# Turning all of B by transposing transfers in halves, moving two small loads to ScalarE's queue, and a new instruction order, in a kernel of two sequence layers

## The chip, the cores and the metric

The kernel runs on one core of one Trainium2 chip. The metric is the device time of one execution in microseconds (us); the figure given for a kernel is the median of its runs.

Engines are called PE (TensorE), DVE (VectorE), ACT (ScalarE), POOL (GpSimd) and SP (SyncE, whose queue issues most transfers). PEld is PE's loading of weights.

## What is computed

Two layers over 2048 positions and 640 channels, all in bf16, written side by side into one output of 2048 x 1280.

```python
# layer A: a diagonal complex recurrence
Lam_bar = exp(exp(log_dt) * Lam)
B_bar   = ((Lam_bar - 1) / Lam)[:, None] * (B_re + 1j * B_im)
Bu      = einsum("bld,pd->blp", x, B_bar)
for t in range(2048):  h = Lam_bar * h + Bu[:, t];  hs.append(h)
y_A     = 2 * real(einsum("blp,dp->bld", hs, C_re + 1j * C_im)) + x * Dskip

# layer B: a short convolution, a gate, a convolution as long as the sequence, a gate
kv  = (sum over t of 4 shifts of k times shift_k) * v
y   = irfft(rfft(kv, 4096) * rfft(ssm_k, 4096))[:2048] + kv * ssm_D
y_B = q * y
```

## The kernel before, in words

**Layer A.** The 640 states are five blocks of 128, called j = 0 to 4; the 640 channels are five blocks too. Time is split into T = 8 phases c of M = 256 columns. x is loaded transposed, one transfer for each phase (`load_x`, L445), into tiles xT; phase c and phase c + 4 share a tile. B is needed transposed as well, in the tile BT with 2 parts (real r = 0, imaginary r = 1), five channel blocks and 640 state columns. For a block j the items `u1j`, `u3j` (phases 1 and 5, 3 and 7; one item for each part r), `vj` (phases 2 and 6), `wj` (phase 4) and `zj` (phase 0) multiply xT by BT on PE (L460, L468) and add, through small diagonal matrices diagL that hold powers of Lam_bar (L474, L475), what earlier phases gave. The results stand in PSUM and are copied into the tiles u by DVE (L148) or ACT (L146). After `zj` the scan `rsj` runs on DVE (L496, between rotations L487 to L489), then `roj`, then the seven other phases get the scanned state back: `mcj` multiplies (L316 on DVE, L314 on ACT) and `rcj` adds on DVE (L522). Last, 32 halves `pn_b` multiply the states by C on PE (L532). For n = 0, 1, 2 the skip term x * Dskip is added on PE, for the other 13 DVE adds it (L560, L547). Results go out from the tile yo.

**The parameters of layer A** come from four short loads on ACT's queue (`lv`, L151), one matmul that turns them (`pv`, L255), and long chains of five-column instructions on DVE: `rho`, `Fi` (to L280), `lam` (L293 to L310), and `gam` (L332 to L346). `dLj` builds diagL of block j, nine instructions.

**How B gets into BT.** Block 0 (128 rows, parts re and im) is loaded as it lies by two plain transfers on ACT's queue (`B0`, L155) into a corner of the tile zz. PE turns it by ten matmuls with the identity (`bt0_0`, `bt0_1`, L431 and L432), and DVE copies the result from PSUM into BT (`bte0_0`, `bte0_1`, L148). Blocks 1 and 2, and blocks 3 and 4, come by transposing transfers on SP's queue (`turn_B`, L167; items `B1` and `B3`, each a real and an imaginary transfer of 256 rows).

**Layer B** works in five groups G of 128 channels. For a group: k and v are loaded transposed (`kTG`, `vTG`, L584), a copy of k with halves exchanged is made (`ksG_h`, L148 or L146 into kS), the four taps run on PE (`tapG_m`, L617) with diagonals made from shift_k (`sk`, `dSG`), DVE multiplies by v (`kvG_m`, L622), the product goes out to DRAM and comes back in rows (`kvoG`, L625; `kvsG`, L595 into kv_st), and the filter's rows come in as `hsG` (L595 into h_st), to which DVE adds ssm_D (`hadG`, L601). Then three stages of a Fourier transform on PE with copies from PSUM between: `s1`, `s2` (L654), a complex product on DVE (`yG_h`, L668 to L671, some 3.8 us each), `inv` (L682), a turning transfer (`ztG`, L690), `fin` (L704), the gate on DVE (`obG`, L709) and the way out (`odG`).

**What sets the order.** There is no scheduler at run time. `make_plan` lists every item with engine, operands and a cost; a string ORDER, found beforehand from those costs, gives the order in which the items are issued, the pair of PSUM banks that an item uses (`@0` to `@7`), and for the copies and scalings that both can do, whether DVE (`v`) or ACT does them. Each engine and each queue runs its items strictly in that order and waits at each for its operands.

```python
    for n, _, how in names:              # names: ORDER.split()
        it = items[n]
        if it["eng"] == "AD":
            args.append("DVE" if how.endswith("v") else "ACT")
        ...
        it["fn"](*args)
```

Four warm-up items `wm0` to `wm3` (L422, four matmuls of 512 columns each with no use for their result) keep PE busy before operands come. Matrix C is loaded by two transposing transfers (`CT0`, `CT1`, L802) into Cs and scaled by `gam` in `caj` on ACT and `csj` on DVE. The vector ssm_D comes by two transfers on SP's queue into the zeroed tile dst (`dcol`, L570), and the taps shift_k by one (`l_sk`, L170).

Of the kernel before, what the change touches and what calls it, by code (L numbers as in the profile page):

```python
# [48 lines left out]
class Kernel:  # L49


    def __init__(self, ctx, tc, out, ins):
# [111 lines left out]
    def turn_B(self, j, n):  # L164
        s = slice(128 * j, 128 * j + 128 * n)
        for r, ap in enumerate((self.A_B_re, self.A_B_im)):
            self.nc.sync.dma_start_transpose(out=self.BT[:, r, :, s], in_=ap[s, :].rearrange("m (k d) -> m k d", d=128))  # L167
# [256 lines left out]
    def pe_bt(self, js, ks, ps):  # L424
        mm = self.nc.tensor.matmul
        i = 0
        for j in js:
            for k in ks:
                re, im = (self.Bn[:, r, j, 128 * k:128 * k + 128] for r in range(2))
                o_re, o_im = (ps[:, r, 128 * i:128 * i + 128] for r in range(2))  # L430
                mm(o_re, lhsT=re, rhs=self.ident[:], start=True, stop=True)  # L431
                mm(o_im, lhsT=im, rhs=self.ident[:], start=True, stop=True)  # L432
                i += 1

    def ev_bt(self, eng, js, ks, ps):
        n = len(js) * len(ks)
        if len(js) == 1:
            out = self.BT[:, :, ks[0]:ks[-1] + 1, 128 * js[0]:128 * js[0] + 128]
            self.copy(eng, out, ps[:, :, 0:128 * n].rearrange("p r (k n) -> p r k n", n=128))
        else:  # L440
            self.copy(eng, self.BT[:, :, ks[0], 128 * js[0]:128 * js[-1] + 128], ps[:, :, 0:128 * n])


# [580 lines left out]
```

## Time and profile before

| | |
|---|---|
| time of the kernel | median 194.97 us of 3 runs (194.75 to 196.81) |
| the profiled execution | 194.97 us, span 192.7 us |
| PE busy | 179.6 us (93%) |
| DVE busy | 175.0 us (91%) |
| ACT busy | 154.2 us (80%) |
| POOL busy | 20.0 us (10%) |
| SP's queue q1, packets' time as a share of 16 engines' span | 92.1% |
| transferred | 34.87 MB, mean 181 GB/s |

The span runs from the first instruction to the last; about 2.3 us of the execution lie around it. A row of a timeline gives the start, the length, the engine, the line, the operation, what it writes and reads, its shape, how many were merged, and in brackets how long the engine idled before it and what ended that. A row of the windows gives the stretch, its length, then busy time and count of instructions for PE, PEld, DVE, ACT and POOL, the clock granted to PE as a share of the full one, the share of time in which the transfer engines were busy, and GB/s. Rows of the issuing queue (SPq, ACTq) show how long the issue took, not when the data landed.

### The profile page before, as it was taken

What the parts mean: (1) busy time and instruction counts of PE and PEld (TensorE: products, weight loads), DVE (VectorE), ACT (ScalarE), POOL (GpSimd) and SP (SyncE); (2) the same over time, 40 slices, a digit from 0 to 9 for tenths busy, and PEclk for the clock granted to TensorE, in tenths of its full rate; (3) what the DMA queues carried; (4) which work ended last, traced back from release to release, by engine and by line L of the source; (5) the groups of instructions that cost most, each with busy time, mean ns of one, the idle gap of its engine ahead of it and who ended that gap; (6) DMA issues with size and microseconds to landing.
All of it is one profiled execution on the core that took longest, in us unless ns stands there. A gap on an engine that the chain in (4) does not pass through costs nothing. (4 is left out here: it accounts for less than half of the span.)

```text
span 192.7 us, 7254 instructions
## 1 busy us (share of the span) xinstructions
PE 179.6 (93%) x3135; PEld 121.6 (63%) x3135; DVE 175.0 (91%) x375; ACT 154.2 (80%) x220; POOL 20.0 (10%) x46
## 2 busy tenths in 40 slices
PE   6499999999898999999899997999999999999993
PEld 2334456556454668576565886787686878777761
DVE  2398799999999999999999999999999999999683
ACT  2648998999999999989899999899989968670000
POOL 8792283000000000000000000000000000000000
PEclk9859999999999999999999999999999999999999
DMA  4999999999999998999979998599935597359954
GB/s 92 183 200 155 190 175 235 229 151 246 189 168 248 177 218 147 156 266 205 189 127 178 126 280 201 111 170 176 228 106 143 114 193 234 102 151 230 256 157 135
DMA packets 131966, 34.87 MB, mean 181 GB/s; under 512 B 127200, under 2 KB 131296, under 8 KB 131936
## 3 DMA queue, kind: packets, MB, share of 16 engines
q1 hardware_dynamic: 131608, 34.10, 92.1%
q10 hardware_dynamic: 328, 0.33, 1.1%
q8 instruction: 24, 0.39, 0.8%
q14 instruction: 6, 0.05, 0.1%
HBM read 10.50 MB, written 7.86 MB: 95 GB/s over the span
## 5 line engine op out<-in xcount | busy, mean ns | idle before, releaser
L532 PE MATMUL banks<-Cs,u 128*128 128x320 bf16 x320 | 46.2, 299 | 0.3 <-DVE yo L547 0.3
L146 ACT CAST XH<-banks 128x1024 bf16<-128x1024 f32 x40 | 39.1, 1032 | 5.3 <-PE banks L654 5.3
L532 PEld LDWEIGHTS <-u 128*128 128x128 bf16 x320 | 30.2, 98 | 12.8 <-issue 0.5
L146 ACT CAST As<-banks 128x1024 bf16<-128x1024 f32 x38 | 37.6, 1043 | 0.8 <-PE banks L636 0.8
L460 PE MATMUL banks<-xT,BT 128*128 128x512 bf16 x150 | 37.4, 392 | 0.6 <-DVE u L148 0.6
L522 DVE TENSOR_TENSOR u<-tmp,u 128x1024 bf16<-128x1024 bf16 (+1 forms) x40 | 24.5, 623 | 1.0
L460 PEld LDWEIGHTS <-BT 128*128 128x128 bf16 x150 | 13.7, 100 | 17.9 <-issue 2.9
L146 ACT CAST u<-banks 128x512 bf16<-128x512 f32 x29 | 16.8, 594 | 6.0 <-PE banks L460 3.5
L146 ACT CAST zz<-banks 128x1024 bf16<-128x1024 f32 x20 | 20.2, 1035 | 1.6 <-PE banks L682 1.6
L654 PE MATMUL banks<-As,Gre 64*64 64x256 bf16 x320 | 19.4, 274 | 1.2 <-DVE As L148 0.8
L654 PE MATMUL banks<-As,Gim 64*64 64x128 bf16 x320 | 18.0, 216 | 0.0
L654 PE MATMUL banks<-As,nGim 64*64 64x128 bf16 x320 | 18.0, 216 | 0.0
L475 PE MATMUL banks<-u,diagL 128*128 128x256 bf16 (+1 forms) x60 | 15.9, 291 | 0.0
L474 PE MATMUL banks<-u,diagL 128*128 128x256 bf16 (+1 forms) x60 | 15.9, 290 | 0.0
L468 PE MATMUL banks<-xT,BT 128*128 128x256 bf16 x100 | 14.2, 273 | 0.7 <-DMA xT<-in_A_x_dram 0.6
L654 PEld LDWEIGHTS <-Gre 64*64 64x64 bf16 x320 | 10.2, 106 | 6.2 <-issue 4.0
L316 DVE TENSOR_SCALAR tmp<-u,lam 128x512 bf16<-128x512 bf16 (+2 forms) x45 | 13.7, 363 | 0.2
L709 DVE TENSOR_TENSOR qb<-banks,qb 128x1024 bf16<-128x1024 f32 x10 | 11.9, 1216 | 1.5 <-PE banks L704 1.5
L669 DVE TENSOR_TENSOR XH<-XH 128x2048 bf16<-128x2048 bf16 x10 | 12.2, 1225 | 0.4
L547 DVE TENSOR_TENSOR yo<-banks,BT 128x320 bf16<-128x320 f32 x26 | 11.8, 486 | 0.7 <-PE banks L532 0.2
L668 DVE TENSOR_TENSOR tmp<-XH 128x2048 bf16<-128x2048 bf16 x10 | 12.2, 1220 | 0.2
L622 DVE TENSOR_TENSOR vT<-banks,vT 128x1024 bf16<-128x1024 f32 x10 | 12.1, 1221 | 0.1
...
## 6 DMA issues: line engine op xcount, KB each, us to landing
...
```

What stands on the lines that cost most here:

```text
L146: self.nc.scalar.copy(out=out, in_=in_)
L316: self.nc.vector.tensor_scalar_mul(out=out, in0=in_, scalar1=w)
L460: self.nc.tensor.matmul(ps, lhsT=self.BT[:, r, k, j * 128:(j + 1) * 128], rhs=x[:, :, k, :], start=(k == 0), stop=(not joins and k == NT - 1))
L468: self.nc.tensor.matmul(o, lhsT=self.BT[:, r, k, j * 128:(j + 1) * 128], rhs=self.xc(c)[:, k, :], start=(k == 0), stop=False)
L474: mm(o, lhsT=self.dl(j)[:, 3 * s, :], rhs=src(c2, r), start=False, stop=False)
L475: mm(o, lhsT=self.dl(j)[:, 3 * s + 2 - r, :], rhs=src(c2, 1 - r), start=False, stop=(i == len(joins) - 1))
L522: v.tensor_tensor(out=o, in0=buf[:, i, 0:n], in1=o, op=ALU.add)
L532: mm(ps[:, 0:320], lhsT=h[:, r, ts], rhs=self.Cs[:, r, j, c0:c0 + 320], start=(j == 0 and r == 0), stop=(skip and j == NT - 1 and r == 1))
L622: self.nc.vector.tensor_tensor(out=self.vT[:, ts], in0=ps[:].rearrange("p a n -> p (a n)"), in1=self.vT[:, ts], op=ALU.mult)
L654: mm(out, lhsT=w[rows, k, :], rhs=rhs, start=(w is self.Gre), stop=(w is self.Gim))
L668: tt(out=cr, in0=X[:, :, ::-1, :], in1=pl(2, 3).to_broadcast([128, 8, 2, 128]), op=ALU.mult)
L669: tt(out=X, in0=X, in1=pl(0, 1).to_broadcast([128, 8, 2, 128]), op=ALU.mult)
```

## The change

Three things. B comes by transposing transfers alone: blocks 0 and 1, blocks 2 and 3, and block 4, each as one transfer for the real and one for the imaginary part, six items `Bj_r` on SP's queue; the ten matmuls, the two copies, the plain loads and their corner of zz are gone. A pair item of part r now waits for the transfers of its own part alone. The loads of shift_k and ssm_D are issued by ACT's queue. And the planner's costs were set anew (among them `rate=0.245` for transposing transfers, and higher costs of `Fi`, `lam`, `gam` and `dL`), and ORDER is a new one throughout. The choice of the three outputs whose skip term PE adds is written as a tuple `PD = (0, 1, 2)` in place of a count, with the same three.

```diff
-JB = 1
 NYO = 4
-NSK = 13
+PD = (0, 1, 2)
...
-    def turn_B(self, j, n):
+    def turn_B(self, j, n, r):
         s = slice(128 * j, 128 * j + 128 * n)
-        for r, ap in enumerate((self.A_B_re, self.A_B_im)):
-            self.nc.sync.dma_start_transpose(out=self.BT[:, r, :, s], in_=ap[s, :].rearrange("m (k d) -> m k d", d=128))
+        self.nc.sync.dma_start_transpose(out=self.BT[:, r, :, s],
+                                         in_=(self.A_B_re, self.A_B_im)[r][s, :].rearrange("m (k d) -> m k d", d=128))
...
-    def pe_bt(self, js, ks, ps):
...
-    def ev_bt(self, eng, js, ks, ps):
...
-        dma(name, "SP", cost, mb, deps, fn, lat=2.1, rate=0.228)
+        dma(name, "SP", cost, mb, deps, fn, lat=2.1, rate=0.245)
...
-    dma("B0", "ACT", 0.9, 0.36, ["lv"], lambda: K.load_B(nc.scalar, 0))
-    for j in (1, 3):
-        dmat(f"B{j}", 2.8, 0.655, (), lambda j=j: K.turn_B(j, 2))
+    for j, n in ((0, 2), (2, 2), (4, 1)):
+        for r in range(2):
+            dmat(f"B{j}_{r}", 1.45 if n == 2 else 1.3, 0.1638 * n, (), lambda j=j, n=n, r=r: K.turn_B(j, n, r))
...
-    dma("l_sk", "SP", 0.75, 0.06, (), lambda: K.load_sk(nc.sync))
+    dma("l_sk", "ACT", 0.65, 0.06, ["lv"], lambda: K.load_sk(nc.scalar))
...
-    dma("dcol", "SP", 1.0, 0.01, ["zd"], lambda: K.load_dcol(nc.sync))
+    dma("dcol", "ACT", 1.25, 0.01, ["zd", "lv"], lambda: K.load_dcol(nc.scalar))
...
-            pe(f"{nm}_{r}", n * P512, 2 * n, deps, lambda ps, r=r: K.pe_u(j, c, r, joins, ps), f"H{nm}_{r}")
+            pe(f"{nm}_{r}", n * P512, 2 * n, [d for d in deps if d[0] != "B" or d[-1] == str(r)], lambda ps, r=r: K.pe_u(j, c, r, joins, ps), f"H{nm}_{r}")
...
-        bt = [f"bte{j}_{x}" for x in range(2)] if j < JB else [f"B{(j - 1) // 2 * 2 + 1}"]
+        bt = [f"B{j // 2 * 2}_{r}" for r in range(2)]
...
-zer x5 pc lv B0 pc3 zd x7 pc2 dc wm1@0 gp0 wm3@2 wt dc2 pp pv@4 exp@4 vec@4 dD wm2@6 rho Fi gp2 bt0_0@0 rr trig1 hk tp0 tab0
...
+x1 zer pc dc lv pc3 x5 pc2 wm2@0 wm0@2 B0_0 wt B0_1 pv@4 exp@4 x7 zd wm1@6 dcol x3 wm3@0 dc2 i64 pp vec@4 hk rho rr pp2 Fi trig1
```

What the new order does is seen in the built programs, at three places. The first is the start of SP's queue, the transfers in the order of their issue. Tile xT_130 holds phases 1 and 5, xT_132 phases 3 and 7, xT_131 phases 2 and 6, xT_129 phases 0 and 4; dst belongs to ssm_D, sk_b to shift_k. Before:

```order
L445 DMA_TRANSPOSE xT_130<-in_A_x_dram 128x5x256
L445 DMA_TRANSPOSE xT_132<-in_A_x_dram 128x5x256 x2
L570 DMA dst<-in_B_ssm_D_dram 2x5x64 x2
L445 DMA_TRANSPOSE xT_130<-in_A_x_dram 128x5x256
L167 DMA_TRANSPOSE BT<-in_A_B_re_dram 128x5x256
L167 DMA_TRANSPOSE BT<-in_A_B_im_dram 128x5x256
L445 DMA_TRANSPOSE xT_131<-in_A_x_dram 128x5x256 x2
L445 DMA_TRANSPOSE xT_129<-in_A_x_dram 128x5x256
L584 DMA_TRANSPOSE kT<-in_B_k_dram 128x2048
L170 DMA sk_b<-in_B_shift_k_dram 128x5x4
L584 DMA_TRANSPOSE vT<-in_B_v_dram 128x2048
L445 DMA_TRANSPOSE xT_129<-in_A_x_dram 128x5x256
```

Now (the line numbers are those of the changed file):

```order
L419 DMA_TRANSPOSE xT_130<-in_A_x_dram 128x5x256 x2
L160 DMA_TRANSPOSE BT<-in_A_B_re_dram 128x5x256
L160 DMA_TRANSPOSE BT<-in_A_B_im_dram 128x5x256
L419 DMA_TRANSPOSE xT_132<-in_A_x_dram 128x5x256 x2
L160 DMA_TRANSPOSE BT<-in_A_B_im_dram 128x5x256
L419 DMA_TRANSPOSE xT_131<-in_A_x_dram 128x5x256 x2
L419 DMA_TRANSPOSE xT_129<-in_A_x_dram 128x5x256
L160 DMA_TRANSPOSE BT<-in_A_B_re_dram 128x5x256
L558 DMA_TRANSPOSE kT<-in_B_k_dram 128x2048
L558 DMA_TRANSPOSE vT<-in_B_v_dram 128x2048
L419 DMA_TRANSPOSE xT_129<-in_A_x_dram 128x5x256
```

Blocks 0 and 1 of B stand third and fourth, blocks 2 and 3 follow around phases 2, 6 and 4, and phase 0 of x, the last row of both, has four B transfers ahead of it where there were two and loads of dst and sk_b.

The second place is the same queue just behind, as far as the second load of kT (h_st: the filter's rows; kv_rows: the product on its way out; kv_st: the same coming back in rows; Cs: matrix C). Before:

```order
L595 DMA h_st<-in_B_ssm_k_dram 64x32x64 x2
L584 DMA_TRANSPOSE kT<-in_B_k_dram 128x2048
L625 DMA kv_rows<-vT 128x2048
L167 DMA_TRANSPOSE BT<-in_A_B_re_dram 128x5x256
L167 DMA_TRANSPOSE BT<-in_A_B_im_dram 128x5x256
L584 DMA_TRANSPOSE vT<-in_B_v_dram 128x2048
L595 DMA kv_st<-kv_rows 64x32x64 x2
L584 DMA_TRANSPOSE kT<-in_B_k_dram 128x2048
```

Now:

```order
L569 DMA h_st<-in_B_ssm_k_dram 64x32x64 x2
L768 DMA_TRANSPOSE Cs<-in_A_C_re_dram 128x5x640
L599 DMA kv_rows<-vT 128x2048
L558 DMA_TRANSPOSE kT<-in_B_k_dram 128x2048
L768 DMA_TRANSPOSE Cs<-in_A_C_im_dram 128x5x640
L558 DMA_TRANSPOSE vT<-in_B_v_dram 128x2048
L569 DMA kv_st<-kv_rows 64x32x64 x2
L558 DMA_TRANSPOSE kT<-in_B_k_dram 128x2048
L160 DMA_TRANSPOSE BT<-in_A_B_im_dram 128x5x128
```

Both parts of C come ahead of the first kv_st, where two transfers of B stood; before, C came after the second kv_st.

The third place is DVE between the end of `Fi` and the start of `lam`. Before:

```order
L279 TENSOR_SCALAR fr<-fr 128x5
L280 CAST Fi<-fr 128x5
L148 CAST BT<-banks 128x2x128
L148 CAST BT<-banks 128x2x4x128
L293 TENSOR_TENSOR lam<-rr,cos_86 128x5
```

Now:

```order
L273 TENSOR_SCALAR fr<-fr 128x5
L274 CAST Fi<-fr 128x5
L146 CAST u_134<-banks 128x2x256
L287 TENSOR_TENSOR lam<-rr,cos_86 128x5
L288 TENSOR_TENSOR lam<-rr,sin_84 128x5
```

Two copies of turned B into BT stood ahead of `lam`; now one copy of the first u item does.

More of the change, by code (lines that the diff above doesn't have):

```diff
@@ L422, in pe_warm @@
             self.nc.tensor.matmul(ps[:, i % 2, :], lhsT=self.ident[:], rhs=wide, start=True, stop=True)
-    def pe_bt(self, js, ks, ps):
[L425 to L433, printed above, removed]
-    def ev_bt(self, eng, js, ks, ps):
[L436 to L441, printed above, removed]
     def load_x(self, c):
@@ L549, in xr @@
     def xr(self, n):
-        return self.BT[:, 0, n % NXR, :]
+        return self.BT[:, 0, [k for k in range(16) if k not in PD].index(n) % NXR, :]
     def load_xr(self, c, i, n):
@@ L762, in make_plan @@
     dve("vec", 0.3, ["pv", "exp"], lambda ps: K.dve_vec(ps), give="pv")
-    dve("rho", 0.4, ["exp", "vec"], lambda: K.dve_rho())
+    dve("rho", 0.7, ["exp", "vec"], lambda: K.dve_rho())
     act("rr", 0.25, ["rho"], lambda: K.act_rr())
-    dve("Fi", 1.3, ["rho"], lambda: K.dve_Fi())
-    act("trig1", 2.1, ["Fi", "rr", "dc"], lambda: K.act_sincos())
-    dve("lam", 3.6, ["trig1", "rr"], lambda: K.dve_lam())
-    dve("gam", 1.8, ["lam"], lambda: K.dve_gamma())
+    dve("Fi", 1.9, ["rho"], lambda: K.dve_Fi())
+    act("trig1", 1.6, ["Fi", "rr", "dc"], lambda: K.act_sincos())
+    dve("lam", 4.8, ["trig1", "rr"], lambda: K.dve_lam())
+    dve("gam", 2.7, ["lam"], lambda: K.dve_gamma())
     gp("pc2", 1.6, ["pc"], lambda: K.pool_consts2())
@@ L786, in make_plan @@
         dve(f"nG{q}", 0.27, [f"G{q}"], lambda q=q: K.dve_nG(q))
-    bts = [(j, ks) for j in range(JB) for ks in ([0, 1, 2, 3], [4])]
-    for j, ks in bts:
-        x = int(ks[0] == 4)
-        w = len(ks)
-        pe(f"bt{j}_{x}", 2 * w * P128, 4 * w, ["dc", f"B{j}"],
-           lambda ps, j=j, ks=ks: K.pe_bt([j], ks, ps), f"bt{j}_{x}")
-        ev(f"bte{j}_{x}", 256 * w, [f"bt{j}_{x}"], lambda eng, ps, j=j, ks=ks: K.ev_bt(eng, [j], ks, ps), f"bt{j}_{x}")
-    bts_all = [f"bt{j}_{x}" for j in range(JB) for x in range(2)]
     gp("hk", 0.9, ["dc2"], lambda: K.pool_hk())
@@ L846, in make_plan @@
     zs_all = [n for j in range(NT) for n in both(f"u1{j}") + both(f"u3{j}") + both(f"v{j}") + [f"w{j}", f"z{j}"]]
-    if NSK:
+    if len(PD) < 16:
         dma("dbc", "SP", 0.5, 0.107, zs_all, lambda: K.load_dbc())
     seq = [(c, i) for c in (0, 4, 2, 6, 1, 5, 3, 7) for i in range(2)]
+    sk = [n for n in range(16) if n not in PD]
     for n, (c, i) in enumerate(seq):
         hs = [f"r{'o4'[c // 4] if c % 4 == 0 else c % 4}{j}" for j in range(NT)]
-        skip = n >= 16 - NSK
+        skip = n not in PD
         free = f"yd{n - NYO}" if n >= NYO else f"cs{NT - 1}"
         if skip:
-            dma(f"xl{n}", "SP", 0.43, 0.107, both(f"ye{n - NXR}") if n >= 16 - NSK + NXR else zs_all, lambda c=c, i=i, n=n: K.load_xr(c, i, n))
+            dma(f"xl{n}", "SP", 0.43, 0.107, both(f"ye{sk[sk.index(n) - NXR]}") if sk.index(n) >= NXR else zs_all, lambda c=c, i=i, n=n: K.load_xr(c, i, n))
             dve(f"xm{n}", 0.4, [f"xl{n}", "dbc"], lambda n=n: K.dve_xm(n))
```

80 lines of the change are left out of this document (38 added, 42 removed).

## Prediction

> **What bounds the kernel now.** I read the busy time by stretches first, then the timelines of DVE, PE and SP's queue. In the windows the columns after the length are PE, PEld, DVE, ACT and POOL, then PE's clock, the transfer engines' share and GB/s:
>
> ```profile
> 24.00:181.00 157.00, 151.69 (x2890) 107.35 (x2888) 153.14 (x278) 139.09 (x186) 5.61 (x9) 1.00 0.97 185
> ```
>
> For 157 us PE, DVE, ACT and the transfers are all close to full; DVE is the fullest, 153.1 of 157. Its timeline shows no wait above the view's threshold inside; these are the last wait ahead of the full stretch, the first instruction of the first scan, the last residual add, and the first wait behind:
>
> ```profile
> 23.86 0.80 DVE L148 COPY kS<-kT 64x1032 bf16<-64x1032 bf16 x1 [0.65 <-DMA kT<-in_B_k_dram]
> ...
> 33.02 0.42 DVE L487 TENSOR_TENSOR tmp<-tab,u 128x512 bf16<-128x512 bf16 x1
> ...
> 174.35 1.41 DVE L522 TENSOR_TENSOR u<-tmp,u 128x1024 bf16<-128x1024 bf16 x2
> ...
> 182.47 2.36 DVE L709 TENSOR_TENSOR qb<-banks,qb 128x1024 bf16<-128x1024 f32 x2 [1.50 <-PE banks L704]
> ```
>
> So three parts set the end: when the scan can start (33.02), how much DVE has to do from there to the last add (it ends at 175.8), and what PE has left then. The wait at 182 belongs to the tail, where PE is the bound.
>
> Ahead of 24 us the bound is what arrives. PE's start:
>
> ```profile
> 1.55 3.25 PE L422 MATMUL banks<-ident 128*128 128x512 bf16 x8 [1.55 <-DVE m_lo L207]
> ...
> 8.68 0.29 PE L432 MATMUL banks<-ident,zz 128*128 128x128 bf16 x1 [1.20 <-DMA zz<-in_A_B_im_dram]
> ...
> 11.47 10.31 PE L460 MATMUL banks<-xT,BT 128*128 128x512 bf16 x40
> ...
> 29.18 0.72 PE L468 MATMUL banks<-xT,BT 128*128 128x256 bf16 x5 [0.55 <-DMA xT<-in_A_x_dram]
> ```
>
> The first useful matmul stands at 11.47, behind the turning of block 0; at 29.18 z0 had waited 0.55 us for phase 0 of x. The first row also tells that the warm-up ran slowly: 8 matmuls of 512 columns in 3.25 us, 406 ns each. PE's clock, by stretches:
>
> ```profile
> 0.90:4.31 3.41, 2.76 (x7) 1.04 (x8) 0.92 (x15) 0.79 (x1) 3.33 (x14) 1.00 0.52 112
> 4.31:7.72 3.41, 1.68 (x8) 0.50 (x6) 0.95 (x6) 1.68 (x6) 3.01 (x9) 1.00 1.12 172
> 7.72:11.13 3.41, 2.45 (x13) 1.38 (x13) 2.23 (x8) 3.35 (x11) 2.40 (x5) 0.50 0.94 198
> 11.13:14.55 3.42, 3.42 (x9) 1.15 (x9) 3.38 (x18) 0.81 (x4) 3.25 (x5) 0.50 1.06 194
> ```
>
> The clock was half from 7.72 to 14.55 (and by the 406 ns also before 4.31, though no record says so). A stretch of 3.41 us with PE busy 81% (2.76) was followed by the full clock, one with 49% by the half, one with 72% (2.45) by the half again.
>
> **Block 0 of B off PE.** Ten matmuls and two DVE copies go (1215 and 425 ns, below). PE need not wait for them: the real half of blocks 0 and 1 is third in SP's queue.
>
> ```profile
> 3.85 2.91 SPq L445 DMA_TRANSPOSE xT<-in_A_x_dram  x1
> ...
> 6.88 1.29 SPq L570 DMA_DIRECT2D dst<-in_B_ssm_D_dram  x2
> ...
> 21.25 0.59 SPq L170 DMA_DIRECT2D sk_b<-in_B_shift_k_dram  x1
> ```
>
> The third transfer of before was issued at 3.85. The view of tile xT has the landing:
>
> ```profile
> DMA to landing us min/median/max: 5.0/5.2/6.7
> ```
>
> That makes 8.9 to 9.1. The plain load of block 0 ran beside it then:
>
> ```profile
> q10 hardware_dynamic: 328, 0.33, 1.1%
> ```
>
> 1.1% of 192.7 us is 2.1 us of all engines' time, which frees up. So the first u item starts between 7 and 9 us; the warm-ups last until about 8.3, and I take 8.7. PE is then busy for some 3.0 us of the stretch from 7.72 to 11.13, 88%, and I take the full clock from 11.13. Between the first u item and z0 PE had 17.2 us before (11.47 to 28.63, where z0's wait begins), 1.5 of it lost to the clock: 15.7 of work. Now two u halves more stand ahead of z0, (10.31 - 1.5) / 8 = 1.1 each, so 17.9 of work; 1.2 is lost to the clock. PE comes to z0 at 8.7 + 19.1 = 27.8. DVE's chain `lam` does not gain: the first u copy (686 ns) stands ahead of it and ends near 8.7 + 5 x 0.42 + 0.7 = 11.5, where before the copies of B ended at 11.4; its diagonals are needed by v0 only, at about 21, which hides it. Were that cover gone, v0 would slip by the 0.2 us.
>
> **When phase 0 of x lands.** Two more transposing transfers of 0.33 MB stand ahead of it. Transposes alone ran at
>
> ```profile
> 17.20:21.30 4.10, 4.10 (x21) 1.86 (x19) 3.76 (x28) 4.07 (x8) 0.00 (x0) 1.00 1.04 226
> ```
>
> 226 GB/s, so +2.9 us; the plain load frees 2.1. The two loads that moved to ACT's queue held SP's issue for 1.29 + 0.59 = 1.9 us. What that gave the transfers is between 0 (the engines had work left) and 1.9; I take 1.0, the middle, since the stretch from 6.88 on lay behind transfers still under way. Sum: 29.2 + 2.9 - 2.1 - 1.0 = 29.0, bounds 28.1 and 30.0. On ACT's queue the loads cost the same 1.9 us, ssm_D's ahead of `rr`, which waits for `rho` anyway, shift_k's ahead of copies that PE's slower start delays.
>
> The Trainium skill (DMA: Bandwidth & Descriptors, "Issuing engines are not separate DMA queues") says that transfers issued by several engines share the same 16 transfer engines and that spreading them saves issue time only. By that alone the sum would be 30.0; the transfer share of 0.97 above agrees with it.
>
> So z0 starts at 29.0, by its operand, and not by PE (27.8). The scan stood 3.84 us behind z0's start, of which DVE's own work held the last 0.6, for the copy of z0 ended at 32.4:
>
> ```profile
> 31.80 0.58 ACT L146 CAST u<-banks 128x512 bf16<-128x512 f32 x1 [0.74 <-PE banks L475]
> ```
>
> Now DVE has less ahead of the scan (next part), so 29.0 + 3.2 = 32.2: **-0.8 us**.
>
> **What DVE has to do.** By the order's rows, with these durations:
>
> ```profile
> L148 DVE CAST u<-banks 128x512 bf16<-128x512 f32 x11 | 7.4, 686 | 0.9 <-PE banks L460 0.5 <-ACT Gre L142 0.4
> ...
> L148 DVE COPY kS<-kT 64x1032 bf16<-64x1032 bf16 x7 | 3.3, 477 | 0.8 <-DMA kT<-in_B_k_dram 0.6
> L148 DVE CAST As<-banks 128x1024 bf16<-128x1024 f32 x2 | 2.5, 1226 | 0.1
> ...
> L148 DVE CAST BT<-banks 128x1024 bf16<-128x1024 f32 x1 | 1.2, 1215 | 0.0
> ...
> L148 DVE CAST BT<-banks 128x256 bf16<-128x256 f32 x1 | 0.4, 425 | 1.0 <-PE banks L432 1.0
> ```
>
> and of the timeline
>
> ```profile
> 36.84 0.74 DVE L316 TENSOR_SCALAR tmp<-u,lam 128x512 bf16<-128x512 bf16 x3
> ...
> 38.99 1.01 DVE L316 TENSOR_SCALAR tmp<-u,lam 128x1024 bf16<-128x1024 bf16 x3
> ...
> 47.28 1.55 DVE L316 TENSOR_SCALAR diagL<-ident,lam 128x128 bf16<-128x128 bf16 x9
> ```
>
> Over the whole kernel DVE loses the two copies of B (1.6), six u copies (4.1), two long and one short set of scalings (2.0 + 0.7), and gains three kS copies (1.4), one set of diagL (1.6) and one copy out of PSUM of 1024 columns (1.2): 4.2 us net, all but the first shifted to ACT or taken from it; ACT's 139 of 157 us leave room for that. But nearly all of it goes ahead of the scan: there the two B copies, two u copies and some smaller ones go, a kS copy and the diagL come, about 3 us less. From the scan to the last add four copies (-2.7) and the scalings (-2.7) go, and two kS copies, one copy of 1024 columns and five smaller ones of 0.3 to 0.9 come (+5.1): **-0.3 us**. The 3 us ahead of the scan are hidden by the wait for x, and count only if x comes earlier.
>
> **The tail.** Behind the last add PE had (175.8 to 189.4) 13.6 us: eight halves and both blocks of `fin4`.
>
> ```profile
> 181.22 2.21 PE L704 MATMUL banks<-Mq,zz 128*64 128x64 bf16 x128
> 183.37 4.25 PE L532 MATMUL banks<-Cs,u 128*128 128x320 bf16 x30
> 187.89 1.52 PE L532 MATMUL banks<-Cs,u 128*128 128x320 bf16 x10 [0.27 <-DVE yo L547]
> ```
>
> In the new order eight halves and one block of `fin4` are left behind it, 2.21 / 2 = 1.1 less: **-1.1 us**.
>
> **C moved forward** on SP's queue.
>
> ```profile
> 32.39 1.85 SPq L167 DMA_TRANSPOSE BT<-in_A_B_re_dram  x1
> 34.29 1.66 SPq L167 DMA_TRANSPOSE BT<-in_A_B_im_dram  x1
> ...
> 39.41 2.92 SPq L595 DMA_DIRECT2D kv_st<-kv_rows  x2
> ...
> 55.26 4.93 SPq L802 DMA_TRANSPOSE Cs<-in_A_C_re_dram  x1
> ...
> 60.88 5.50 SPq L802 DMA_TRANSPOSE Cs<-in_A_C_im_dram  x1
> ```
>
> The first kv_st is first read at 45.6, and the first DVE copy of what PE makes of it starts at 49.28:
>
> ```profile
> L636 PE MATMUL banks<-R,kv_st x160: 212/216/227, 45.6 to 150.5; 64*128 64x128 bf16 x160
> ```
>
> ```profile
> 49.28 1.23 DVE L148 CAST As<-banks 128x1024 bf16<-128x1024 f32 x1
> ```
>
> That is 16.3 us behind the scan. In the new order DVE has 1.4 us more in between (both scalings of C's first blocks, less other work), so it comes there at 32.2 + 17.7 = 49.9. By issue times kv_st is 4.93 + 5.50 - 3.51 - 0.2 = 6.7 us later, read from 52.3; by bytes (1.64 MB of C, 0.66 of B, at 226 GB/s) 4.3 - 0.2 later, 49.7. So DVE waits between 0 and 2.4 us; the issue times hold waits of their own, so I take the middle, **+1.2 us**. What is queued behind that instruction on DVE is the next kS copies and the scan of block 1.
>
> **Sum:** -0.8 - 0.3 - 1.1 + 1.2 = -1.0, from 194.97 of the profiled execution, which is also the median: 194.0.
>
> **Rivals.** *Faster, 191.9.* C's transfers fit (no wait) and x comes at 28.1, since the queue runs unbroken; DVE, with 3 us less ahead of the scan, and PE (27.8) are ready by then. The scan stands at 31.3: -1.7 - 0.3 - 1.1 = -3.1. For it speaks the 226 GB/s; against it the mean of 185 over the full stretch. *Slower, 198.0.* C ahead of the first group's transfers keeps the queue late from 36 us until the place where C stood before, 66 us, so DVE meets kv_st, the second kT and the second h_st late one after another: the wait is the whole 6.7, less 0.2 to 2 made up by work that is ready, 5.2 instead of 1.2. It decides as soon as kv_st is read after 53. Against it: DVE has scalings of C to do meanwhile. *No earlier start, 195.0.* The half clock lasts to 14.55 as before (loss 2.9 for 1.2) and PE reaches z0 at 29.5, x lands at 30.0: the scan stands at 33.2, so +0.2 - 0.3 - 1.1 + 1.2 = 0.0.
>
> The Trainium skill (TensorE: Matmul & The Clock Gate, "What's actually happening") has the clock released after a busy window of about 3.4 us that runs freely. By that rule taken strictly, the stretch to 11.13 is not wholly busy, which is the case just named. The trace agrees on the length (3.41) and not on strictness (81% sufficed); the phase of the window may differ from run to run.
>
> **Chances.** Forecast 0.34, no earlier start 0.12, faster 0.33, slower 0.21. A measurement of this kernel tells about 1% from no change, so the first two are "same". The forecast's own range, with x at 28.1 to 30.0 or the wait at 0 to 2.4, one at a time, is 192.8 to 195.2; the range that reaches into both other cases is 190.6 to 198.2.
>
> **What would show it.** Right: first L460 matmul near 8.7 and full clock from 11.13; z0 near 29.0, waiting for xT; the scan near 32.2; DVE with a wait for PE's L636 or for kv_st between 45 and 53; a wait-free DVE behind. Wrong: a scan before 31 with no wait near 50 (faster); several DVE waits on transfers between 40 and 66 (slower); and waits on DVE behind 70 us, of which nothing here speaks, since I have followed the new order by place only up to there and at the tail.

## The result and the profile after

| | before | changed |
|---|---|---|
| median of the timed runs | 194.86 us (4 runs, 193.74 to 196.81) | 202.36 us (4 runs, 201.24 to 202.39) |
| profiled execution, span | 194.97, 192.7 us | 202.36, 200.1 us |
| first scan starts | 33.02 | 40.26 |
| from there to the end of the span | 159.7 | 159.8 |

The changed kernel is slower: ratio 1.037, 95% interval 1.033 to 1.041. Forecast were 194.0 us and a first scan at 32.2. All but 0.2 us of the loss stands ahead of the first scan. The ratios here and below leave out executions over 1.5% above the fastest of the same kernel (among the experiments two of kernel 8's four and one of kernel 2's, the profiled one), while the medians count all of them.

The page's busy times of the changed kernel show no engine with more work:

```profile
PE 179.3 (90%) x3125; PEld 120.6 (60%) x3125; DVE 172.2 (86%) x371; ACT 155.3 (78%) x222; POOL 19.1 (10%) x46
```

DVE's timeline has the same marks as before: the first instruction of the first scan, the last residual adds, the first wait behind them.

```profile
40.26 0.42 DVE L461 TENSOR_TENSOR tmp<-tab,u 128x512 bf16<-128x512 bf16 x1
...
181.51 2.88 DVE L496 TENSOR_TENSOR u<-tmp,u 128x1024 bf16<-128x1024 bf16 x4
...
189.28 2.36 DVE L683 TENSOR_TENSOR qb<-banks,qb 128x1024 bf16<-128x1024 f32 x2 [1.39 <-DMA qb<-in_B_q_dram]
```

Scan to last add takes 144.1 us (before 142.7), the rest 15.7 (before 16.9). What is late is found on ACT. In its timeline, rows marked ACTq are transfers that it issues:

```profile
5.58 0.18 ACT L252 ACTIVATE dt_b<-banks 128x5 bf16<-128x5 f32 x1 [1.68 <-PE banks L249]
10.11 2.30 ACTq L544 DMA_DIRECT2D dst<-in_B_ssm_D_dram  x2
12.45 0.21 ACT L277 ACTIVATE rr<-rho 128x5 f32<-128x5 f32 x1 [6.69 <-DMA xT<-in_A_x_dram]
...
21.20 0.40 ACTq L164 DMA_DIRECT2D sk_b<-in_B_shift_k_dram  x1
21.65 1.57 ACT L308 ACTIVATE diagD<-ident,vec 128x128 bf16<-128x128 bf16 x5 [4.73 <-DMA xT<-in_A_x_dram]
23.13 2.01 ACT L144 CAST u<-banks 128x512 bf16<-128x512 f32 x4
```

ACT stood still for 6.69 us ahead of `rr` and 4.73 ahead of `diagD` (the issues of 2.30 and 0.40 us are within these figures), each time right where it had a small load to issue, and each time what ended the wait was the landing of a phase of x, which neither instruction reads. The built program tells why: the transfers that SP and ACT issue take eight semaphores in rotation to report their landing, and before one of them is issued, the earlier transfer that had the same semaphore must have landed. In the changed kernel these rows stand on ACT:

```
L544 DMA dst<-in_B_ssm_D_dram 2x5x64 [waits DMAHW7_49,Pool_49]
L544 DMA dst<-in_B_ssm_D_dram 2x5x64 [waits DMAHW0_49]
L277 ACTIVATE rr<-rho 128x5 [waits DVE_49]
...
L164 DMA sk_b<-in_B_shift_k_dram 128x5x4 [waits DMAHW5_49]
L308 ACTIVATE diagD<-ident,vec 128x128 x5
```

Counting round the eight, 7 had last been given to the imaginary part of blocks 0 and 1 of B, 0 to phase 7 of x, 5 to phase 4 of x, whose issue ended on SP at 17.88. On SP, where the small loads stood before, no such gap shows: by the prediction's rows the issue ahead of ssm_D's ended at 6.76 and ssm_D's began at 6.88. Behind the loads on ACT stand `rr`, the sines and the u copies. Who waits for these, by the list of waits (total, times, longest):

```profile
DVE sk_b L168 <- DMA sk_b<-in_B_shift_k_dram: 6.1, 1, 6.1
PE banks L434 <- ACT u L144: 5.6, 1, 5.6
...
DVE lam L287 <- ACT cos L140: 3.3, 1, 3.3
```

`lam` is 3.3 us late. The u copies come at 23.13, PSUM banks stay full until then, and PE, which had begun as forecast, stops:

```profile
8.49 2.33 PE L434 MATMUL banks<-xT,BT 128*128 128x512 bf16 x10 [1.12 <-DMA BT<-in_A_B_re_dram]
...
23.74 5.84 PE L434 MATMUL banks<-xT,BT 128*128 128x512 bf16 x15 [5.61 <-ACT u L144]
...
36.35 0.72 PE L442 MATMUL banks<-xT,BT 128*128 128x256 bf16 x5
```

The last row is z0: it starts at 36.35 without a wait for x (forecast: PE there at 27.8, x at 29.0). Which of ACT's two waits held it, the chain of work tells that is followed back from the end of the program, each piece to what released it (start, length, what):

```profile
15.90 5.28 DMA xT<-in_A_x_dram
...
21.20 0.40 ACTq L164
...
21.65 1.57 ACT diagD L308 x5
23.22 0.48 ACT u L144
...
23.74 5.84 PE banks L434 x15
```

Ahead of these stand only SP's own issues, one behind the other; phase 4 of x lands at 21.18, and the issue of the taps' load, `diagD`, the first u copy and PE follow. The wait of ssm_D's loads, over at 12.45, is not on the chain, and neither is `lam`. PE's stop also cost clock. In the windows, PE's busy time is the first figure behind the length, its clock the third from the end:

```profile
8.00:14.00 6.00, 4.96 (x22) 2.07 (x23) 3.12 (x7) 1.52 (x3) 5.65 (x8) 1.00 1.17 191
...
18.00:24.00 6.00, 0.39 (x2) 0.10 (x1) 1.43 (x9) 2.35 (x7) 0.00 (x0) 0.82 1.26 206
24.00:31.00 7.00, 7.00 (x23) 2.71 (x22) 4.17 (x17) 5.67 (x11) 0.00 (x0) 0.66 1.23 190
```

Full clock early on, then 0.66 behind the idle stretch.

### The profile page after: what moved, and what is told of

It is laid out like the page before. It is cut to its first block, busy times and chain, and to the rows that moved or that the text cites. A ratio compares the mean times of both kernels' runs of the same rounds, so it can differ in the third digit from the quotient of the medians.

```text
span 200.1 us, 7238 instructions
## 1 busy us (share of the span) xinstructions
PE 179.3 (90%) x3125; PEld 120.6 (60%) x3125; DVE 172.2 (86%) x371; ACT 155.3 (78%) x222; POOL 19.1 (10%) x46
## 4 chain that ended last, share of the span: by engine, by line
PE 43%; DVE 29%; ACT 8%; SPq 7%; DMA 6%; issue 4%; ACTq 0%; DVEq 0%
PE banks L506 21%; SPq L419 5%; PE banks L434 5%; PE banks L678 4%; PE banks L656 4%; DMA kv_st<-kv_rows 4%; DVE vT L596 3%; DVE XH L643 3%; DVE tmp L642 3%; ACT XH L144 3%; PE banks L628 3%; DMA xT<-in_A_x_dram 3%; SPq L160 3%; DVE u L496 2%; PE banks L591 2%
## 5 line engine op out<-in xcount | busy, mean ns | idle before, releaser
L434 PE MATMUL banks<-xT,BT 128*128 128x512 bf16 x150 | 38.7, 399 | 8.1 <-ACT u L144 5.6
L496 DVE TENSOR_TENSOR u<-tmp,u 128x1024 bf16<-128x1024 bf16 (+1 forms) x40 | 25.0, 632 | 1.2
L144 ACT CAST u<-banks 128x512 bf16<-128x512 f32 x35 | 20.2, 605 | 3.1 <-PE banks L449 1.8
L144 ACT CAST zz<-banks 128x1024 bf16<-128x1024 f32 x19 | 19.3, 1039 | 2.5 <-PE banks L656 2.5
L308 ACT ACTIVATE tmp<-u,lam 128x512 bf16<-128x512 bf16 (+2 forms) x24 | 18.1, 843 | 0.0
L656 PE MATMUL banks<-XH,I 64*128 64x128 bf16 x320 | 11.5, 217 | 1.7 <-DVE vT L596 1.0
```

The lines of the kernel that those rows point to most:

```text
L144: self.nc.scalar.copy(out=out, in_=in_)
L308: self.nc.scalar.activation(out=out, in_=in_, func=ACT.Copy, scale=w)
L434: self.nc.tensor.matmul(ps, lhsT=self.BT[:, r, k, j * 128:(j + 1) * 128], rhs=x[:, :, k, :], start=(k == 0), stop=(not joins and k == NT - 1))
L496: v.tensor_tensor(out=o, in0=buf[:, i, 0:n], in1=o, op=ALU.add)
L656: self.nc.tensor.matmul(out, lhsT=w, rhs=rhs, start=(pl == 1), stop=(pl == 2))
```

## The experiments

**The theory** was that ACT's waits for landings cost the time, and that with them gone the forecast's 194 comes back. **Rivals**: the new order, with C forward on SP's queue, costs it; B as transposes brings operands late; one of the two loads alone counts. Each ratio is to the kernel before on the same chip, whose median was 194.86 us beside the changed kernel and 196.0 to 196.7 beside the others. The chips differ by 1 to 2 us, so ratios are compared, not times; 1 to 4 ran on one chip, 5 to 8, 9 to 11, and 12 and 13 on others, and the changed kernel on none of these.

| kernel | median us | ratio, 95% interval | first scan |
|---|---|---|---|
| changed | 202.36 | 1.037, 1.033 to 1.041 | 40.26 |
| 1 both loads on SP | 199.93 | 1.018, 1.010 to 1.026 | 35.98 |
| 2 taps on ACT, ssm_D on SP | 200.30 | 1.015, 1.006 to 1.024 | 36.41 |
| 3 ssm_D on ACT, taps on POOL | 198.55 | 1.011, 1.004 to 1.018 | 34.99 |
| 4 taps on ACT, ssm_D on POOL | 198.77 | 1.011, 1.005 to 1.017 | 35.78 |
| 5 both on POOL | 199.64 | 1.018, 1.013 to 1.023 | 35.10 |
| 6 old order, both on ACT | 201.07 | 1.023, 1.017 to 1.029 | 37.87 |
| 7 old order, B alone | 197.24 | 1.005, 1.002 to 1.007 | 35.03 |
| 8 as 5, second pair of B late | 201.06 | 1.016, 1.011 to 1.022 | 35.75 |
| 9 as 5, dL2 behind the scan | 198.80 | 1.013, 1.006 to 1.019 | 33.87 |
| 10 as 1, second pair of B late | 198.97 | 1.013, 1.006 to 1.020 | 30.82 |
| 11 old order, second pair late | 200.23 | 1.019, 1.012 to 1.026 | 34.59 |
| 12 as 1, C late | 205.47 | 1.050, 1.044 to 1.057 | 35.80 |
| 13 as 10, C late | 204.82 | 1.045, 1.038 to 1.053 | 31.91 |

### Both loads back on SP, and on POOL (1 and 5)

```diff
-    dma("l_sk", ... lambda: K.load_sk(nc.scalar))
+    dma("l_sk", ... lambda: K.load_sk(nc.sync))        # in 5: nc.gpsimd
-    dma("dcol", ... lambda: K.load_dcol(nc.scalar))
+    dma("dcol", ... lambda: K.load_dcol(nc.sync))      # in 5: nc.gpsimd
```

> The changed kernel with both small loads (taps of shift_k, columns of ssm_D) issued by SP again, the rest of the change kept. Theory (ACT, strictly in order, stands still at each of the two loads until a bulk transfer has landed; in the changed kernel 6.7 us ahead of rr and 4.7 us ahead of diagD): both waits of ACT are gone, lam starts at 11 to 12 us instead of 14.6, PE does not wait 5.6 us in u31_0, the first scan starts at 32 to 33.5 instead of 40.3, time 194 to 195.5 (the prediction's 194.0, at most 1.0 more since SP's issue holds the loads again). Rival A (the new order, or C forward on SP's queue, costs the time): scan still near 40, time over 200. Rival B (block 0 of B as transposes brings B or x late): scan at 36 or later, time over 198.

> The changed kernel with both small loads issued by GpSimd: neither ACT nor SP holds them. After the first runs the theory has two layers: ACT's waits set the scan at 40.3; with them gone it stands at 35 to 36.4, set by the arrival of phase 0 of x (30.9 to 31.3) and of h_st (DVE waits about 1 us for it) behind the B transposes on SP's queue, and by the 1.5 us of scalings of lam that DVE has ahead of the scan in the new order. Theory: no wait of ACT for a landing, x phase 0 some 1 us earlier than with both on SP (30 to 30.5), scan at 34 to 35, ratio to the kernel before 1.00 to 1.012. Rival (it is the issue by ACT or SP that counts and nothing else holds): scan at 32 to 33, ratio under 0.995.

Kernel 1's timeline of ACT has `rr` five us earlier, and no wait for a landing:

```profile
7.43 0.21 ACT L277 ACTIVATE rr<-rho 128x5 f32<-128x5 f32 x1 [1.57 <-DVE rho L263]
...
13.62 1.56 ACT L308 ACTIVATE diagD<-ident,vec 128x128 bf16<-128x128 bf16 x5
```

The scan came 4.3 us earlier, the ratio fell from 1.037 to 1.018, and the intervals do not meet. So by these ratios, from two chips, ACT's waits cost about half of the loss; profiles on one chip, further down, give less. But 194 did not come back, and the scan stood at 36.0, not 32 to 33.5: the theory held for one layer, and a second lay beneath it. Rival B's signs, a scan at 36 or later and over 198 us, all but came out (35.98 and 199.93). Kernel 1's z0 (PE), and its DVE ahead of the scan:

```profile
31.30 0.72 PE L442 MATMUL banks<-xT,BT 128*128 128x256 bf16 x5 [0.28 <-DMA xT<-in_A_x_dram]
```

```profile
34.39 0.30 DVE L575 TENSOR_TENSOR h_st<-h_st,dcol_b 128x32 bf16<-128x32 bf16 x1 [1.02 <-DMA h_st<-in_B_ssm_k_dram]
34.52 1.54 DVE L310 TENSOR_SCALAR diagL<-ident,lam 128x128 bf16<-128x128 bf16 x9
35.98 0.42 DVE L461 TENSOR_TENSOR tmp<-tab,u 128x512 bf16<-128x512 bf16 x1
```

Phase 0 of x, behind the added transposes, lands at 31.3, h_st later still (DVE waits 1.02 us), and 1.54 us of scalings stand between them and the scan. With both on POOL z0 stood at 30.86 and the scan at 35.1, just outside what was expected, and the ratio was no better, 1.018 where 1.00 to 1.012 was expected.

### Is it the queue, or whose landing is waited for? (2)

```diff
-    dma("dcol", ... lambda: K.load_dcol(nc.scalar))
+    dma("dcol", ... lambda: K.load_dcol(nc.sync))
```

> The changed kernel with only the columns of ssm_D issued by SP again; the taps of shift_k stay on ACT's queue, at the same place. The order's waits show that the taps' load now waits for the semaphore on which the ssm_D columns landed last, long before, and not for a phase of x. Theory (it is the landing of the transfer that used the same semaphore eight transfers earlier that holds ACT, not the load or its queue): no wait of ACT above 1 us ahead of diagD, scan at 32 to 34, time within 1 us of the kernel with both on SP. Rival C (a load from ACT's queue is slow in itself, or stands behind the bulk transfers): ACT idle for 4 us or more ahead of diagD again, PE waits in u31_0, scan at 36 to 38, time 198 to 200.

The taps stay on ACT's queue at the same place. With ssm_D back on SP their turn among the eight semaphores has changed, to one whose last transfer, a load of ssm_D, landed long before. ACT in this kernel:

```profile
13.37 0.40 ACTq L164 DMA_DIRECT2D sk_b<-in_B_shift_k_dram  x1
13.81 1.57 ACT L308 ACTIVATE diagD<-ident,vec 128x128 bf16<-128x128 bf16 x5
```

The load issues at once and takes 0.40 us; the 4.73 us are gone, and the time is that of kernel 1. Beyond those 0.40 us neither the queue nor the load is seen to cost ACT anything: the landing does that the load must wait for. Rival C falls. The scan, expected at 32 to 34, stood at 36.41, held by the second layer like kernel 1's.

### One load alone on ACT (3 and 4)

```diff
-    dma("l_sk", ... lambda: K.load_sk(nc.scalar))      # in 3
+    dma("l_sk", ... lambda: K.load_sk(nc.gpsimd))
-    dma("dcol", ... lambda: K.load_dcol(nc.scalar))    # in 4
+    dma("dcol", ... lambda: K.load_dcol(nc.gpsimd))
```

> The changed kernel with only the taps of shift_k taken off ACT (issued by GpSimd, whose transfers wait for none of these semaphores); the columns of ssm_D stay on ACT's queue and wait for the same two transfers as in the changed kernel. Theory: rr waits 6 to 7 us again and lam 3.3, but diagD does not wait; PE's wait ahead of u31_0 falls from 5.6 to 1 or 2, scan at 34 to 36, time 195.5 to 198. Rival D (only the ssm_D columns count, everything later follows from lam being late): scan at 39 to 40, time 201 to 202. Rival E (only the taps count): time as with both on SP.

> The changed kernel with only the columns of ssm_D taken off ACT (issued by GpSimd); the taps of shift_k stay on ACT's queue, and by the order's waits they now wait for the landing of phase 2 of x, which landed some 2 us before phase 4 in the changed kernel. Theory: rr and lam are on time (lam at 11 to 12), ACT is idle for 3 to 5 us ahead of the taps' load until 18 to 19 us, PE waits 2 to 4 us in the u items, scan at 34.5 to 37, time 196.5 to 199. Rival E (only the taps count) gives 199 or more, rival D (only the ssm_D columns count) the time with both on SP.

The waits in kernel 3, then in kernel 4:

```profile
ACT rr L277 <- DMA xT<-in_A_x_dram: 7.5, 1, 7.5
```

```profile
ACT diagD L308 <- DMA xT<-in_A_x_dram: 6.4, 1, 6.4
```

and, in the timeline of kernel 4, the issue of the taps:

```profile
17.48 0.40 ACTq L164 DMA_DIRECT2D sk_b<-in_B_shift_k_dram  x1
```

The waits of ACT are there as expected, 7.5 and 6.4 us, and yet both kernels are as fast as those without any (1.011, their intervals overlap those of 1 and 5), with scans at 35.0 and 35.8. So each of these waits is hidden beneath the second layer, x and h_st, that holds the scan at 35 to 36 anyway. Rival D falls: ssm_D's wait alone costs nothing. Rival E, that only the taps count, does not: kernel 3, with the taps off ACT, is as fast as the kernels with both loads off it, which is what E gives. Kernel 4 does not refute it, since its taps wait for another landing, phase 2 of x, and are issued at 17.48; in the changed kernel they wait for phase 4 until 21.20. That is 3.7 us later, and its scan stands 4.5 later (40.26 against 35.78). With the chain above this says that the taps' wait cost the time, by when it ended and not by its length; that both waits together are needed is not shown. ssm_D's loads mattered in that they moved the taps' turn among the semaphores (kernel 2).

### Each part alone in the old order (6 and 7)

```diff
-    dma("l_sk", ... lambda: K.load_sk(nc.sync))        # 6: the kernel before with this
+    dma("l_sk", ... lambda: K.load_sk(nc.scalar))
-    dma("dcol", ... lambda: K.load_dcol(nc.sync))
+    dma("dcol", ... lambda: K.load_dcol(nc.scalar))
```

```diff
-zer x5 pc lv B0 pc3 zd x7 pc2 dc wm1@0           # 7: pieces of ORDER
+zer x5 pc lv pc3 zd x7 B0_1 B0_0 pc2 dc wm1@0
-gp2 bt0_0@0 rr
+gp2 rr
-bt0_1@2 bte0_1@2v wm0@4 hp0 x3 bte0_0@0v u30_1@0
+wm0@4 hp0 x3 u30_1@0
-dL1@v B1
+dL1@v B2_0 B2_1
-B3 v1e_0@3
+B4_0 B4_1 v1e_0@3
```

> The kernel before with one part of the change alone: the two small loads on ACT's queue, at the places that the old order gives them. By the order's waits each again waits for the landing of a bulk transfer (the ssm_D columns for two, the taps for one). Theory: ACT stands still for several us ahead of them and PE waits for its u copies; slower than before by 2 to 6 us (ratio 1.01 to 1.03), scan at 35 to 39. Rival (the old order has other work on ACT while they wait, so they cost nothing, and only the new order makes them dear): ratio 0.995 to 1.005.

> The old order with the B part of the change alone: block 0 of B by transposing transfers in real and imaginary halves of blocks 0 and 1, 2 and 3, 4; no turning on PE, no copies of it; the small loads stay with SP. Block 0 and 1's halves stand behind x phases 5 and 7 in SP's queue, the others where the pairs of blocks stood. Theory: two more transposes ahead put phase 0 of x 1 to 3 us later (30 to 32), z0 follows it, scan at 34 to 36, ratio 1.003 to 1.015. Rival (B as transposes is free, the new order is what costs in the kernels with both loads off ACT): ratio 0.99 to 1.002.

The loads alone make the old kernel 2.3% slower. ACT in kernel 6:

```profile
15.94 2.68 ACTq L570 DMA_DIRECT2D dst<-in_B_ssm_D_dram  x2
18.66 0.26 ACT L141 ACTIVATE yo<-yo 128x64 f32<-128x64 int32 x1 [6.51 <-DMA xT<-in_A_x_dram]
...
27.12 0.38 ACTq L170 DMA_DIRECT2D sk_b<-in_B_shift_k_dram  x1
```

Here ACT stands still once, 6.51 us; the taps are issued without a wait, but only at 27.12, behind all that was held up. They land at 31.3, DVE waits 4.3 us for them, and z0, which stands behind the matmuls of the taps on PE, starts at 34.32. So a single wait is enough if the taps come late by it. B alone costs 0.5%: its z0 waits for x until 31.48, its scan stands at 35.03.

```profile
31.48 0.72 PE L442 MATMUL banks<-xT,BT 128*128 128x256 bf16 x5 [1.51 <-DMA xT<-in_A_x_dram]
```

### What the kernels without ACT's waits still pay (8 to 13)

> The changed kernel with both loads issued by GpSimd, and the second pair of B (blocks 2 and 3) behind phase 0 of x and h_st on SP's queue instead of ahead; the two u items that need it on PE behind z0; one set of scalings of lam on DVE behind the first scan instead of ahead. Theory: x phase 0 lands 3 us earlier (27 to 28), h_st too, z0 at 28 to 29, scan at 31.5 to 33, ratio 0.985 to 0.998; what is moved behind the scan costs at most 1 us there. Rival (the rest behind the scan takes back what is gained ahead, since PE and DVE are both over 94% busy there): ratio 1.0 or more with the scan early.

> The kernel with both small loads on GpSimd, with one thing changed: the scalings of lam for block 2 (dL2, 1.5 us on DVE) stand behind the first scan instead of ahead of it. Theory (what counts is how long DVE idles ahead of the first scan, 21 to 23 us in the kernels with the loads off ACT against 17.7 before, and not where the scan stands among DVE's work): the scan moves to 33.5 to 34, and the time stays within 0.6 us of the same kernel with dL2 ahead, ratio 1.012 to 1.02. Rival (work ahead of the scan delays everything behind it): 1.5 us less, ratio 1.007 to 1.012.

> The changed kernel with both small loads on SP, blocks 2 and 3 of B behind phase 0 of x and h_st on SP's queue, and the three u items and copies that need them behind the v items of block 1 on PE, so that the taps' product on DVE stands ahead of them (in the trial before it was held 5.8 us by them). Theory (arrival of x phase 0 and h_st holds the rest): z0 at 27 to 28.5, scan at 30.5 to 32.5, DVE idle 3 to 4 us less, ratio 0.985 to 1.003. Rival (idle time of DVE comes back behind the scan, because the u items of block 2 are late for its chain): ratio 1.005 or more with the scan before 33.

> The old order with block 0 of B by transposing transfers in halves, these first in SP's queue behind x phases 1 and 5, the u items of phase 1 first on PE, blocks 2 and 3 behind phase 0 of x and h_st, both small loads on SP between kT and vT. Theory: PE's first u matmul at 8.5 to 9, phase 0 of x at 26 to 27.5, the two copies of B and one u copy gone from ahead of the scan, DVE has no long wait: scan at 30 to 31.5 instead of about 33, 1.5 to 2.5 us less, ratio 0.985 to 0.993. Rival (GpSimd's work beside DVE stretches lam and its scalings by as much as is gained): scan at 32 to 33, ratio 0.995 to 1.0.

Pieces of ORDER; 9 is the third and the fourth pair of rows alone:

```diff
-aR B2_1 x2                    # 8 and 10; 11 likewise in the old order
+aR x2
-hs0 H1
+hs0 B2_1 B2_0 H1
-s1he0_1@6 dL2@v aM            # 8 to 10
+s1he0_1@6 aM
-kT1 rs0 s1he0_0@6
+kT1 rs0 s1he0_0@6 dL2@v       # in 8 and 9 right behind rs0
-u32_0@2 ze0@1                 # 10; u12_1, u12_0 and the copies of all three too
+ze0@1
-m40@av v1_0@1 r40@a
+m40@av v1_0@1 u32_0@2 u12_1@5 u12_0@3 ... r40@a
```

Kernel 8 was badly built: the moved u items stood ahead of the product with the taps, DVE waited 5.78 us for them, and the run says little. Kernel 11 was slower by 1.9%, outside theory and rival: ahead of its scan DVE waited 3.72 us for ACT, so it says little too. Kernel 9 moved the scan by 1.2 us and the ratio by less than its interval, so its question stays open; the 21 to 23 and 17.7 us of its expectation are DVE's idle time over the whole span (192.7 - 175.0 before), not ahead of the scan. Kernel 10 is the telling one. DVE and PE in it:

```profile
30.82 0.42 DVE L461 TENSOR_TENSOR tmp<-tab,u 128x512 bf16<-128x512 bf16 x1
...
42.54 0.86 DVE L146 COPY kS<-kT 64x1032 bf16<-64x1032 bf16 x2 [1.10 <-DMA kT<-in_B_k_dram]
...
46.25 0.89 DVE L353 SCALAR_TENSOR_TENSOR Cs<-Cs,gam,yo 128x640 bf16<-128x640 bf16 x1 [0.81 <-DMA Cs<-in_A_C_im_dram]
```

```profile
27.58 0.72 PE L442 MATMUL banks<-xT,BT 128*128 128x256 bf16 x5 [0.70 <-DMA xT<-in_A_x_dram]
```

x lands at 27.6 and the scan stands at 30.82, 5.2 us earlier than in kernel 1, as expected; the time hardly moved (1.013 against 1.018), which is what the rival gave. From the scan to the last add it took 149.2 us instead of 145.2: 1.8 more work of DVE (141.96 against 140.13; 1.5 of it the scalings dL2, which the edit moved there), and 2.3 more idle, part of it waits for kT and C. So an early first scan is not worth its microseconds by itself in this order.

That pointed to C ahead on SP's queue, the prediction's slower rival. Kernels 12 and 13 put C behind the second kv_st and its four scalings behind the third scan:

```diff
-ze0@1 CT0
+ze0@1
-tab3 CT1
+tab3
-kvs1
+kvs1 CT0
-kvo2
+kvo2 CT1
-ca0 cs0 ... ca1 ... cs1 ca2 ... cs2 ... ca3
...
-rs2 inv0_2@2 s2e1_3@0 zs0_2@2 zt0_1 s21_4@4 cs3
+rs2 ca0 cs0 inv0_2@2 s2e1_3@0 zs0_2@2 zt0_1 ca1 cs1 s21_4@4 ca2 cs2
```

> The kernel with both small loads on SP (the new order else), with C's two transfers behind the second group's kv_st on SP's queue, and the four scalings of C that need them moved behind the third scan on DVE. Theory (the term C of the prediction, which the ACT waits hid, is what the kernels without ACT waits still pay between the first and the second scan: kv_st, kT and vT stand behind C in SP's queue): the second scan starts 17 to 19 us behind the first instead of 23, and the time falls by 1 to 2.5 us, ratio 1.005 to 1.013 against 1.018 with C ahead. Rival (the scalings fill DVE there, 5.4 us of work that only moves, and no transfer is waited for): ratio 1.015 to 1.022.

> The same move of C in the kernel whose first scan stood at 30.8 (blocks 2 and 3 of B behind phase 0 of x and h_st, both small loads on SP). Theory: there DVE waited 1.1 us for kT, 0.8 for C and the scan gained little; with C late the early scan counts, DVE idles 3 to 5 us less in all than with both loads on SP alone, ratio 0.99 to 1.004. Rival (the order behind the second scan is bound by something else, PE or ACT, and gives back whatever comes early): ratio 1.01 to 1.016, the last add at 180 or later as in the four kernels with scans between 30.8 and 36.

Both were slower than the kernel before by over 4%, outside theory and rival alike. DVE and PE in kernel 12:

```profile
52.90 1.22 DVE L146 CAST As<-banks 128x1024 bf16<-128x1024 f32 x1 [1.89 <-PE banks L610]
...
57.54 0.43 DVE L461 TENSOR_TENSOR tmp<-tab,u 128x512 bf16<-128x512 bf16 x1 [1.81 <-ACT u L144]
```

```profile
87.62 0.43 PE L628 MATMUL banks<-As,Gre 64*64 64x256 bf16 x4 [5.02 <-ACT XH L144]
```

With 5.4 us of scalings taken out between the first and the second scan (three of 1.8), the second came only 1.4 us sooner behind the first (21.7 us against 23.2): DVE then waits for PE and ACT instead (1.89 and 1.81 us). The scalings were filling idle time. Put together later they stop PE for 5.02 us; that loss belongs to where I put them. So C's place is not shown to cost anything in the changed order, and my theory for the rest falls.

### Three profiles on one chip

The kernel before, the changed one and kernel 1, unchanged, one execution each (196.75, 202.00, 200.36 us). A second execution of the kernel before on that chip took 198.30 us, so differences of 1 to 2 us in this part are not clear of noise.

> The kernel before, unchanged, profiled on the same chip as the two kernels behind it, since the chips of the earlier runs differed by 1 to 2 us. Theory: first scan at 33 to 34, DVE idle 8.8 to 10 us ahead of it and 3.3 between it and the last add.

> The changed kernel, unchanged, on that chip. Theory: ACT's two waits of 6 to 8 and 4 to 6 us again, first scan 6.5 to 8 us later than in the kernel before, and the rest of the span the same within 0.7.

> The changed kernel with both small loads on SP, on that chip. Theory: scan 3 to 5 us earlier than in the changed kernel and 2 to 3 later than in the kernel before; of what stays against the kernel before, 2 to 3 us are idle time of DVE ahead of the scan (phase 0 of x 2 us later, h_st behind it), 1 to 2 are idle and longer work behind it, and the tail gives 1 back.

Windows up to the first scan, and from there to the last add; DVE's busy time is the third figure behind the length. The kernel before, the changed one, kernel 1:

```profile
0.00:33.83 33.83, 28.51 (x160) 13.87 (x160) 23.69 (x102) 23.62 (x51) 19.64 (x46) 0.90 0.99 165
33.83:177.35 143.52, 137.91 (x2768) 97.83 (x2769) 139.44 (x253) 130.17 (x170) 0.00 (x0) 1.00 0.94 181
```

```profile
0.00:39.42 39.42, 30.07 (x170) 13.85 (x172) 21.63 (x103) 22.71 (x48) 16.55 (x42) 0.91 0.93 173
39.42:183.73 144.31, 136.35 (x2820) 97.94 (x2815) 139.96 (x249) 132.65 (x175) 2.59 (x4) 1.00 0.90 171
```

```profile
0.00:36.43 36.43, 30.67 (x176) 14.21 (x177) 24.37 (x104) 23.72 (x50) 16.59 (x42) 0.95 0.96 168
36.43:182.49 146.06, 137.48 (x2808) 98.64 (x2807) 140.17 (x249) 131.82 (x173) 2.73 (x4) 0.99 0.94 174
```

Length less DVE's busy time is its idle time. With the spans (194.5, 199.5, 198.0) the differences to the kernel before are:

| | changed | kernel 1 |
|---|---|---|
| DVE idle ahead of the scan (before 10.14) | +7.65 | +1.92 |
| DVE busy ahead of it (23.69) | -2.06 | +0.68 |
| idle, scan to last add (4.08) | +0.27 | +1.81 |
| busy there (139.44) | +0.52 | +0.73 |
| behind the last add (17.15) | -1.38 | -1.64 |
| span | +5.0 | +3.5 |

Against the expectations, the changed kernel's scan came 5.6 us later than that of the kernel before (6.5 to 8 expected), and of what kernel 1 still pays 1.9 us are idle ahead of the scan (2 to 3) and 2.5 idle and longer work behind it (1 to 2). Taking ACT's waits away saves 5.7 us of idle ahead of the scan and gives 4.3 back: 2.7 us more work there, at nearly the same number of instructions, since DVE's instructions get longer (below), and 1.5 more idle behind. By the medians, which rest on more runs but on two chips, 1.9% (some 3.7 us) stay saved; in this single profile of each it is 1.5 us. So the waits cost some 1.5 to 3.7 us, no closer than that, and why DVE idles 1.8 us more behind the scan in kernel 1 than in the kernel before is **not settled**.

## Why the prediction was wrong

**The step that failed** is: "On ACT's queue the loads cost the same 1.9 us, ssm_D's ahead of `rr`, which waits for `rho` anyway, shift_k's ahead of copies that PE's slower start delays." It priced an issue (the rows show 2.30 and 0.40 us for it) and left out what the issue waits for. With it ACT stood still for 6.69 and 4.73 us. `rho` was no cover: without the wait `rr` runs at 7.43, not 12.45, though nothing on the way to the first scan needed it sooner. What counted was the load of shift_k: it could not be issued before phase 4 of x had landed at 21.18, so `diagD` began at 21.65 and the u copies behind it at 23.13, where `diagD` begins at 13.62 without the wait (kernel 1). PE's start was no cover: u results were ready before ACT came, and PE stopped for 5.61 us with its banks full.

**The rivals.** No earlier start (195.0 for a scan at 33.2) was the only one with a later scan, for the wrong reason: it let PE's clock be the cause. No rival named a wait of the loads for other transfers. The slower rival (C keeps the queue late, 198.0) had the sign and not the place.

**Phase 0 of x at 29.0, scan 3.2 behind z0.** In the changed kernel z0 no longer waited for x. Kernel 3 has the same transfers on SP's queue, and there it did:

```profile
30.88 0.72 PE L442 MATMUL banks<-xT,BT 128*128 128x256 bf16 x5 [0.57 <-DMA xT<-in_A_x_dram]
```

So this term was mis-sized as well: 30.9, beyond the bound of 30.0. The forecast gave the loads that left SP 1.0 us of it. On the one chip SP issued phase 0 1.1 us sooner without them (25.08 against 26.19), but it landed only 0.4 sooner (30.88 in kernel 3 against 31.30 in kernel 1). And in kernel 1 the scan followed z0 by 4.7 us, not 3.2, because of h_st and dL2. The claim that DVE has 3 us less to do ahead of the scan held only while ACT's wait kept it off POOL's work (-2.06); without that wait it was +0.68. So even with the loads left on SP the gain ahead of the scan would not have come. As an estimate from these ratios, which come from several chips and need not add up, the loads on ACT's queue make 1.9 of the 3.7% (1.037 to 1.018), B by transposes 0.5 (kernel 7), and the new order 1.3 by difference, whose cause stays open.

**PE's start and clock.** The first u matmul at 8.7: measured 8.49. Full clock from 11.13: it was already full in the stretch from 8.00. The start was right and the clock better than forecast, and both were worthless, as PE then stopped for want of PSUM.

**Behind the scan** the sum was right: -0.2 forecast, +0.2 measured (144.1 and 15.7 us against 142.7 and 16.9). Its terms: scan to last add +0.9 (-0.3 and +1.2), measured +1.4; the tail -1.1, measured -1.2. The wait of 1.2 us for kv_st was not seen as such: the first copy behind it stood 18.7 us after the scan (forecast 17.7 and 1.2 of wait), with no wait of DVE shown, so this term came out near by luck.
